# Attention with a top-32 mask and a routed feed-forward layer: rows scattered straight to their expert's place, and the end of a unit put behind the next search

## The chip, the cores and the metric

The kernel runs on one core of one Trainium2 chip. The metric is device time in microseconds (us) of one execution; the kernel before takes 1912.75 us, the median of three runs (1911.58 to 1913.21). TensorE (PE) multiplies matrices and loads its stationary operand separately (PEld), VectorE (DVE) and ScalarE (ACT) work element by element, GpSimd (POOL) does small work and issues the indirect transfers (scatters and gathers by a list of row numbers), SyncE (SP) issues the plain ones. PSUM is the memory that TensorE writes to.

## The reference

```python
# attention: B, H, S, D = 8, 8, 576, 64
scores = q @ k^T / sqrt(D)
kth = np.partition(scores, -32, axis=-1)[..., -32:-31]   # the 32nd largest of each row
scores = np.where(scores >= kth, scores, -1e9)
attn = softmax(scores)                                   # denominator + 1e-9
x = (attn @ v) laid out as [B*S, H*D] = [4608, 512]
# feed-forward: 8 experts, each row goes to one
logits = x @ w_gate                                      # [4608, 8]
e = argmax(logits, axis=1); gate = softmax(logits)[e]
out = gate * (relu(x @ w1[e]) @ w2[e])                   # w1 [8,512,1024], w2 [8,1024,512]
```

All of it is float32, the scores too, since the mask and the choice of the expert hang on exact comparisons.

## The kernel before, in words

**Attention.** The work goes batch by batch (8), in each batch by unit (4; a unit is a pair of heads), in each unit by group (5: four groups with one tile of 128 queries of either head, and a fifth, half as large, with the last 64 queries of both). One step of the main loop (lines 555 to 572) takes one group: `scores` of the next group (TensorE, copied out of PSUM by ScalarE, line 216), `weights` of this group, `close` of the group before. `weights` is the search: VectorE folds the 576 scores of a row into 288 pairs (`hl`, lines 232 and 233), finds the 32 largest in four rounds of `max` and `match_replace` (lines 240 to 253), and multiplies the exponentials by the mask, with the row sum as a by-product (line 269). The exponentials are ScalarE's (line 244), and their bias `nbias` is -scale times the largest score, a multiplication of two columns on GpSimd (line 242).

`close` transposes the weights on TensorE (`transposed`). With the last group of a unit `outputs` follows: `po`, the product with `v` (line 317), `px` and `pl`, its transposed form and the gate's logits (lines 322 to 335), and then VectorE's part, which scales by the row sums and adds up the logits (lines 302 to 306, and 324 to 347). The transposes, `po`, `px`, `pl` and `rank` all share one pool of two PSUM buffers (`bank`). In the loop the last group of a unit is closed after the search of the next unit's first group.

**Routing.** With the last unit of a batch `route` follows. It finds each row's expert, counts on TensorE (`rank`) how many rows went there before, and so gets a position for each row in its expert's list. Five indirect transfers on GpSimd scatter the row numbers into `lists` in memory (line 382); they write one tensor, and each waits for the one before. The rows of `x`, with the gate's factor as column 513, go to `x_rows` in the order of the tokens, as plain writes (lines 392 and 395). Lists and rows are filled beforehand with a number, or zeros, that stand for "no row".

**Blocks.** A block is 128 list places of one expert. There are 43 block slots. How many are sure to be full after each batch is known beforehand (2, 6, 11, 15, 20, 24 after the second to the seventh batch), and as many are worked on beside the attention of the batch that follows; the last 19 come after all attention. `load_block` loads the list of a block (`idx`, three buffers), the two weight matrices (2 MB each, two buffers each) and gathers the rows by the list (`xg`, two buffers, line 453). It is called for the block two ahead of the one begun. `block` is cut into 17 pieces: transposes of the rows (`xtp`, copied to `xTs`), 8 steps of the first product (`ph`, relu to `hT`), 8 of the second (`py`); at its end ScalarE applies the factor (`y`, line 486), and GpSimd scatters the rows to `out` by the list (line 487).

**Order.** Every engine runs its instructions in the order in which they stand in its queue, and DMAs issued by SP or GpSimd stand in these queues too, with what they wait for. The order is set when the program is built: a scheduler goes by the place of an instruction in the program, and lets later ones go ahead where, by its own durations, an engine would stand. So parts of two groups, or block pieces, stand between each other's instructions, and a wait that it did not foresee holds up all that stands behind.

If some rows can't be decided by the folded search, a second, exact version of everything runs behind the main part (line 585 on); with these inputs it doesn't run.

Of the kernel before, what the change touches and what calls it, by code (L numbers as in the profile page):

```python
# [9 lines left out]
F32 = mybir.dt.float32  # L10
# [3 lines left out]
AX = mybir.AxisListType  # L14

# [24 lines left out]
def kernel(  # L40
# [31 lines left out]

    nc = tc.nc
# [13 lines left out]
    XW = Dm + 1  # L87
    EB = N // P
    NSLOT = EB + E - 1
    LISTB = E * EB + NSLOT  # L90
# [35 lines left out]
    e_at = iota_f("e_at", [P, E], [[N, E]])  # L126
# [4 lines left out]

    tok_id = []
    for b in range(B):
        t = const.tile([P, KC], I32, name=f"tok_id{b}")
        token_ids(t, b)
        tok_id.append(t)
# [23 lines left out]
    lv = lists.rearrange("(r p) o -> p r o", p=P)  # L160
# [58 lines left out]
    def weights(n, tiles, s):  # L219
# [78 lines left out]
    def outputs(n, x, lg):  # L298
# [3 lines left out]
        if not k.exact:  # L302
            nc.vector.tensor_tensor(doubt, doubt, n.over, op=ALU.max)
        nc.vector.tensor_scalar_add(rz[:, 0:NT], n.z, EPS)
        nc.vector.reciprocal(rz[:, 0:NT], rz[:, 0:NT])
        nc.vector.tensor_copy(rz[0:ST, NT:NT + 1], rz[ST:P, NT - 1:NT])
# [12 lines left out]
        rzb = rz[:, :].rearrange("p (t h) -> p t h", h=2)  # L319
# [3 lines left out]
        xu = x[:, :, n.u * P:(n.u + 1) * P].rearrange("p t (h d) -> p t h d", h=2)  # L323
        nc.vector.tensor_tensor(
            xu[:, 0:NC], px[:, :].rearrange("p (t h d) -> p t h d", t=NC, h=2),
            _inner(rzb[:, 0:NC, :], D), op=ALU.mult,
        )
# [3 lines left out]
        for t in range(KC):  # L331
# [4 lines left out]
        nc.vector.tensor_tensor(  # L336
            xu[:, NC], pl[:, 0:P].rearrange("p (h d) -> p h d", h=2), _inner(rzb[:, NC, :], D), op=ALU.mult,
        )
        lt = k.small.tile([P, KC, 2, E], F32, name="lt")
        nc.vector.tensor_tensor(  # L340
            lt, pl[:, P:P + KC * lw].rearrange("p (t h e) -> p t h e", t=KC, h=2), _inner(rzb, E), op=ALU.mult
        )
        if n.u:
            nc.vector.tensor_tensor(lg, lg, lt[:, :, 0, :], op=ALU.add)
            nc.vector.tensor_tensor(lg, lg, lt[:, :, 1, :], op=ALU.add)
        else:
            nc.vector.tensor_tensor(lg, lt[:, :, 0, :], lt[:, :, 1, :], op=ALU.add)
# [309 lines left out]
```

## Time and profile before

| | |
|---|---|
| median of 3 runs | 1912.75 us |
| the profiled execution, its own time | 1911.04 us |
| its span, first to last instruction | 1909.3 us |
| mean granted TensorE clock | 0.825 of 2.4 GHz |
| TensorE busy | 1553.9 us, 81% |
| VectorE busy | 1421.3 us, 74% |
| ScalarE busy | 691.1 us, 36% |
| GpSimd busy | 222.7 us, 12% |
| mean DMA rate | 130 GB/s |

All times of the trace are from the profiled execution. A matmul's busy time includes time in the pipeline, so a busy TensorE is not one at its peak. An instruction's releaser (`<-`) is what it waited for last.

### The profile page before, as it was taken

The numbers are of one execution on the slowest core, as the hardware profiler recorded it, in microseconds if no ns is written. First come the engines' busy times: TensorE is split into PE (matmuls) and PEld (weight loads), VectorE is DVE, ScalarE is ACT, GpSimd is POOL, SyncE is SP. The second block draws the span as 40 slices with busy tenths as digits, with TensorE's granted clock in tenths as the row PEclk, the third lists the DMA queues.
The fourth block names the chain that finished last, engine by engine and source line by source line (L and its number), as shares of the span: only waits on it lengthen the run. The fifth ranks groups of instructions, "written<-read, shape, count | busy, mean of one in ns | idle before, by whom it ended". The sixth has DMA issues, their size and how long they took to land.

```text
span 1909.3 us, 25156 instructions
## 1 busy us (share of the span) xinstructions
PE 1553.9 (81%) x8126; PEld 993.1 (52%) x8126; DVE 1421.3 (74%) x4963; ACT 691.1 (36%) x1269; POOL 222.7 (12%) x471
## 2 busy tenths in 40 slices
PE   5778677877886699769996998599969973999998
PEld 3444344435543466446653664366536552666665
DVE  8999889997999799989997999799988970000000
ACT  3443243434443354434442453345434430111111
POOL 1000100011101110111011010211020101111110
PEclk9765666568956799779985998699959986999999
DMA  9300200015001551156315420644155206979884
GB/s 164 59 20 20 45 20 20 20 45 207 31 20 45 215 179 50 45 207 217 120 52 204 170 81 25 220 170 172 38 177 184 95 7 217 327 261 329 301 294 143
DMA packets 116525, 248.94 MB, mean 130 GB/s; under 512 B 12511, under 2 KB 33119, under 8 KB 116386
## 3 DMA queue, kind: packets, MB, share of 16 engines
q1 hardware_dynamic: 108226, 226.49, 36.5%
q0 software_dynamic: 8160, 20.76, 3.0%
q8 instruction: 67, 1.10, 0.2%
q14 instruction: 72, 0.59, 0.1%
HBM read 221.05 MB, written 28.01 MB: 130 GB/s over the span
## 4 chain that ended last, share of the span: by engine, by line
DVE 45%; PE 26%; DMA 14%; issue 10%; ACT 3%; POOL 2%; SPq 0%; POOLq 0%; DVEq 0%; ACTq 0%
DVE tops L240 13%; DVE scr L250 12%; PE po L317 9%; DVE w L269 7%; DMA out_dram<-y,idx 7%; PE sc L211 5%; PE ph L473 4%; DVE hl L232 3%; DVE tops L247 3%; DVE hl L233 3%; DMA idx<-lists 3%; DMA lists<-tok_id,posi 2%; DMA xg<-x_rows,idx 2%; PE wTm L283 2%; PE py L482 2%
## 5 line engine op out<-in xcount | busy, mean ns | idle before, releaser
L211 PE MATMUL sc<-qkb 64*128 64x288 f32 (+1 forms) x1280 | 379.5, 545 | 9.6 <-DMA qkb<-in_qk_dram 5.7
L473 PE MATMUL ph<-xTs,w 128*128 128x128 f32 x2752 | 348.2, 283 | 27.7 <-ACT xTs L465 27.4
L240 DVE MAX8 tops<-scr 128x8 f32<-128x288 f32 x864 | 356.1, 446 | 1.4
L283 PE MATMUL wTm<-ident,w 128*128 128x128 f32 x1152 | 226.8, 350 | 159.9 <-DVE w L269 150.5
L473 PEld LDWEIGHTS ph<-xTs,w 128*128 128x128 f32 x2752 | 328.7, 197 | 47.4 <-ACT xTs L465 39.8
L482 PE MATMUL py<-w,hT 128*128 128x512 f32 x688 | 315.6, 596 | 0.0
L283 PEld LDWEIGHTS wTm<-ident,w 128*128 128x128 f32 x1152 | 173.6, 180 | 239.3 <-issue 135.0
L244 ACT ACTIVATE w<-s,nbias 128x576 f32<-128x576 f32 x288 | 211.9, 773 | 229.4 <-POOL nbias L242 228.7
L250 DVE MATCH_REPLACE8 scr<-tops,scr 128x288 f32<-128x288 f32 x576 | 250.6, 440 | 0.1
L211 PEld LDWEIGHTS sc<-qkb 64*128 64x128 f32 (+1 forms) x1280 | 179.7, 221 | 130.2 <-issue 62.0
L216 ACT COPY s<-sc 128x576 f32<-128x576 f32 x288 | 174.0, 641 | 193.3 <-DVE w L269 105.8
L269 DVE SCALAR_TENSOR_TENSOR w<-s,thr,w 128x576 f32<-128x576 f32 x288 | 223.7, 807 | 12.5 <-ACT w L244 11.5
L286 ACT COPY wT<-wTm 128x512 f32<-128x512 f32 x256 | 142.7, 591 | 133.8 <-PE wTm L283 133.7
L482 PEld LDWEIGHTS py<-w,hT 128*128 128x128 f32 x688 | 122.3, 190 | 120.5 <-issue 120.3
L317 PE MATMUL po<-wT,vb 128*64 128x288 f32 x1024 | 158.5, 458 | 1.1 <-ACT wT L288 0.9
L232 DVE TENSOR_TENSOR hl<-s 128x576 f32<-128x576 f32 (+1 forms) x160 | 109.5, 685 | 63.9 <-ACT s L216 63.7
L240 DVE MAX8 tops<-hl 128x8 f32<-128x288 f32 x288 | 126.0, 448 | 0.0
L250 DVE MATCH_REPLACE8 scr<-tops,hl 128x288 f32<-128x288 f32 x288 | 125.7, 440 | 0.0
L265 POOL TENSOR_TENSOR over<-tops,thr 128x2 f32<-128x2 f32 (+1 forms) x160 | 36.5, 228 | 746.8 <-DVE thr L264 713.4
L291 PE MATMUL wTl<-ident,w 128*64 128x128 f32 x288 | 76.3, 347 | 55.3 <-ACT wT L286 54.6
L247 DVE MAX8 tops<-hl 128x8 f32<-128x288 f32 x288 | 120.6, 444 | 0.0
L317 PEld LDWEIGHTS po<-wT,vb 128*64 128x64 f32 x1024 | 75.4, 152 | 82.6 <-issue 40.4
(110 smaller groups left out, 1056.1 us busy)
## 6 DMA issues: line engine op xcount, KB each, us to landing
w<-in_moe_w_dram SPq DMA_DIRECT2D x86, 2048.0 KB
qkb<-in_qk_dram SPq DMA_DIRECT2D x32, 576.0 KB
vb<-in_v_dram SPq DMA_DIRECT2D x32, 320.0 KB
x_rows<-x SPq DMA_DIRECT2D x8, 1026.0 KB
x_rows<-zrow SPq DMA_DIRECT2D x1, 6925.5 KB
x_rows<-x SPq DMA_DIRECT2D x8, 128.2 KB
idx<-lists SPq DMA_DIRECT2D x43, 0.5 KB
xg<-x_rows,idx POOLq DMA_INDIRECT x43, 7.3
```

The source lines that it names most:

```text
L211: nc.tensor.matmul(ps[rows, j, 0:HF], n.q[d, cols], n.k[d, j * HF:(j + 1) * HF], start=True, stop=True)
L216: nc.scalar.copy(s[:, m, :, :], ps[:, :, 0:HF])
L232: nc.vector.tensor_tensor(hl[:, 0, m2, :], s[:, m2, 0, :], s[:, m2, 1, :], op=ALU.max)
L240: nc.vector.max(out=tops[:, m, r * 8:(r + 1) * 8], in_=src[m])
L244: nc.scalar.activation(w[:, m, :], flat[m], AF.Exp, scale=scale, bias=nbias[:, m:m + 1])
L247: nc.vector.max(out=tops[:, m, TOP_K + 1:TOP_K + 9], in_=hl[:, 1, m, :])
L250: nc.vector.match_replace(out=scr[:, m, :], in_to_replace=tops[:, m, r * 8:(r + 1) * 8], in_values=src[m], imm_value=NEG,)
L269: nc.vector.scalar_tensor_tensor(out=w[:, m, :], in0=flat[m], scalar=thr[:, m:m + 1], in1=w[:, m, :], op0=ALU.is_ge, op1=ALU.mult, accum_o ...
L283: nc.tensor.transpose(pm[:, c * P:(c + 1) * P], w[:, m, c * P:(c + 1) * P], ident)
L317: nc.tensor.matmul(po[r, 0:HF], lhsT, rhs, start=(c == 0), stop=(c == KC - 1))
L473: nc.tensor.matmul(ph[:, f, :], n.w1[:, 0, dt, fc * P:(fc + 1) * P], xT[:, dt, :], start=(dt == 0), stop=(dt == DT - 1),)
L482: nc.tensor.matmul(py, hT[:, f, :], n.w2[:, 0, f, :], start=(f == 0), stop=(f == FT - 1))
```

## The change

Eight edits.

1. `x_rows` becomes the experts' own stretches: each expert has `CAP` = 4736 rows there. A row has 514 columns: 512 values, the factor, and the number of the token (as an integer). `lists` is gone, and so are the fills at the start.
2. `route` scatters whole rows (five indirect transfers, 128 or 64 rows of 2056 bytes) to their positions. The five are declared independent of one another.
3. `load_block` loads 128 consecutive rows with one plain transfer on SP, which waits for all the scatters. There is no `idx`: the output is scattered by the row tile's last column. The row tile has two buffers, as before.
4. `fill_up`, new, runs after the last batch: one block of blank rows behind each expert's last row, and an `EMPTY` block that the slots past the last are sent to.
5. `outputs` is cut in two: TensorE's and ScalarE's part stays, VectorE's part is returned as `scaled`.
6. `settle`, new, calls `scaled`, and for a batch's last unit `route`, the table of blocks and the loads. The loop calls it right after the next group's `weights` and before `close`, so VectorE's part of a unit comes one search later than before.
7. `nbias` is computed on ScalarE.
8. In the last batch the pieces that are dealt out among the groups leave two blocks (`KEEP`), which come in the program behind the last unit and ahead of the last 19.

```diff
-    XW = Dm + 1
+    XW = Dm + 2
-    LISTB = E * EB + NSLOT
+    CAP = N + P
+    EMPTY = E * CAP // P
...
-    x_rows = dram.tile([N + 1, XW], F32, name="x_rows")
-    lists = dram.tile([LISTB * P, 1], I32, name="lists")
+    x_rows = dram.tile([(EMPTY + 1) * P, XW], F32, name="x_rows")
...
-                nc.gpsimd.tensor_scalar(nbias[:, m2], tops[:, m2, 0], -scale, None, ALU.mult)
+                nc.scalar.mul(nbias[:, m2], tops[:, m2, 0], -scale)
...
-    def outputs(n, x, lg):
+    def outputs(n):
...
+        def scaled(x, lg):
+            if not k.exact:
+                nc.vector.tensor_tensor(doubt, doubt, n.over, op=ALU.max)
+            nc.vector.tensor_scalar_add(rz[:, 0:NT], n.z, EPS)
...
+        return scaled
...
-        for i in range(KC):
-            r = slice(0, P if i < NC else ST)
-            nc.gpsimd.indirect_dma_start(
-                out=lists[:, :], out_offset=bass.IndirectOffsetOnAxis(ap=posi[r, i:i + 1], axis=0),
-                in_=ids[r, i:i + 1], in_offset=None,
-            )
...
-        nc.sync.dma_start(
-            x_rows[bass.ds(row0, SM), :].rearrange("(c p) w -> p c w", p=P), x[:, 0:NC, :]
-        )
-        nc.sync.dma_start(x_rows[bass.ds(row0 + SM, ST), :], x[0:ST, NC, :])
+        mine = []
+        for i in range(KC):
+            r = slice(0, P if i < NC else ST)
+            put = nc.gpsimd.indirect_dma_start(
+                out=x_rows[:, :], out_offset=bass.IndirectOffsetOnAxis(ap=posi[r, i:i + 1], axis=0),
+                in_=x[r, i, :], in_offset=None,
+            ).ins
+            if not k.exact:
+                for other in mine:
+                    tc.declare_no_dep(put, other, reason="the rows of one batch go to different places")
+                mine.append(put)
+        scattered.extend(mine)
+
+    def fill_up():
+        ends = k.small.tile([1, E], I32, name="ends")
+        nc.vector.tensor_copy(ends, run[0:1, :])
+        for e in range(E):
+            r = nc.sync.value_load(ends[0:1, e:e + 1], min_val=e * CAP, max_val=e * CAP + N)
+            put = nc.sync.dma_start(x_rows[bass.ds(r, P), :], blank).ins
+            if not k.exact:
+                for other in scattered:
+                    tc.add_manual_dep(put, other.name, WAIT)
+        nc.sync.dma_start(x_rows[EMPTY * P:(EMPTY + 1) * P, :], blank)
...
-        n.idx = k.mlp.tile([P, 1, 1], I32, name="idx", bufs=3)
-        nc.sync.dma_start(n.idx, lv[:, bass.ds(r, 1), :])
+        n.x = k.mlp.tile([P, 1, XW], F32, name="xg")
+        got = nc.sync.dma_start(n.x, xv[:, bass.ds(r, 1), :]).ins
+        if not k.exact:
+            for put in scattered:
+                tc.add_manual_dep(got, put.name, WAIT)
         n.w1 = k.wp.tile([P, 1, DT, F], F32, name="w1")
...
-        n.x = k.mlp.tile([P, XW], F32, name="xg")
-        nc.gpsimd.indirect_dma_start(
-            out=n.x[:, :], out_offset=None,
-            in_=x_rows[:, :], in_offset=bass.IndirectOffsetOnAxis(ap=n.idx[:, 0, 0:1], axis=0),
-        )
...
         nc.gpsimd.indirect_dma_start(
-            out=out[:, :], out_offset=bass.IndirectOffsetOnAxis(ap=n.idx[:, 0, 0:1], axis=0),
+            out=out[:, :], out_offset=bass.IndirectOffsetOnAxis(ap=n.x[:, 0, Dm + 1:XW].bitcast(I32), axis=0),
             in_=y[:, :], in_offset=None, bounds_check=N - 1, oob_is_err=False,
         )
...
+    FIRST = 5
+    KEEP = 2 * PIECES
...
-            if g != groups[-1]:
+            if g == groups[-1]:
+                late = (b, u, outputs(n))
+
+        def settle():
+            nonlocal late, left
+            if late is None:
                 return
+            b, u, scaled = late
+            late = None
...
-            outputs(n, x_of[b], lg_of[b])
+            scaled(x_of[b], lg_of[b])
             if u < U - 1:
                 return
-            route(x_of[b], lg_of[b], tok_id[b], b * S)
+            route(x_of[b], lg_of[b])
+            if b == B - 1:
+                fill_up()
...
             w = weights(n, g, s_now)
+            settle()
             if last is not None:
                 close(last)
             last = (b, u, g, w)
             at = i % per_batch
-            if at >= 5:
-                pieces(-(-left // (per_batch - at)))
+            if at >= FIRST:
+                rest = left - (KEEP if b == B - 1 else 0)
+                pieces(-(-rest // (per_batch - at)))
         close(last)
+        settle()
         pieces(left)
```

## Rows read from the trace of the kernel before

**Rows 1.** The page: busy time by engine, slices, and the costliest group's line.

```profile
PE 1553.9 (81%) x8126; PEld 993.1 (52%) x8126; DVE 1421.3 (74%) x4963; ACT 691.1 (36%) x1269; POOL 222.7 (12%) x471
...
DVE  8999889997999799989997999799988970000000
...
L211 PE MATMUL sc<-qkb 64*128 64x288 f32 (+1 forms) x1280 | 379.5, 545 | 9.6 <-DMA qkb<-in_qk_dram 5.7
```

**Rows 2.** Stretches from unit to unit: length, busy time (instructions), clock, DMA.

```profile
10.40:57.66 47.26, 31.18 (x98) 17.18 (x96) 47.23 (x159) 19.95 (x36) 2.68 (x11) 1.00 1.01 134
...
150.27:197.02 46.75, 38.39 (x142) 20.94 (x144) 43.36 (x147) 18.41 (x34) 2.44 (x10) 0.57 0.07 20
197.02:252.23 55.21, 34.59 (x147) 19.60 (x148) 45.52 (x167) 18.62 (x35) 8.29 (x15) 0.62 0.18 39
...
651.87:695.49 43.62, 42.78 (x258) 28.05 (x260) 42.74 (x145) 21.39 (x39) 4.69 (x12) 1.00 0.59 202
...
1177.76:1238.28 60.52, 36.63 (x188) 24.49 (x190) 46.63 (x183) 19.68 (x37) 11.86 (x17) 0.66 0.50 161
...
sum 1552.95, PE 1257.83 PEld 781.40 DVE 1411.24 ACT 642.60 POOL 176.87; mean PE 39.31 PEld 24.42 DVE 44.10 ACT 20.08 POOL 5.53
```

**Rows 3.** Waits of VectorE, 10.4 to 1563.35 us: total us, times, longest.

```profile
DVE hl L232 <- ACT s L216: 59.1, 17, 10.2
DVE x L324 <- PE px L322: 47.7, 18, 6.2
DVE w L269 <- ACT w L244: 11.5, 5, 4.2
DVE x L336 <- PE pl L332: 11.0, 22, 1.4
DVE base L367 <- PE rank L363: 4.7, 7, 0.9
```

**Rows 4.** Timeline of GpSimd and ScalarE: first batch's end, start and length.

```profile
236.82 0.92 POOL L382 DMA_INDIRECT lists<-tok_id,posi  x1 [2.04 <-DMA lists<-tok_id,posi]
237.77 0.24 POOL L242 TENSOR_SCALAR nbias<-tops 128x2 f32<-128x2 f32 x1
...
238.04 1.44 ACT L244 ACTIVATE w<-s,nbias 128x576 f32<-128x576 f32 x2 [9.80 <-POOL nbias L242]
```

**Rows 5.** Timeline at the sixth batch's end, all engines.

```profile
1190.47 0.24 ACT L387 ACTIVATE lg<-lg 128x40 f32<-128x40 f32 x1 [2.58 <-DVE lg L386]
...
1196.47 0.17 DVE L379 CAST posi<-posf 128x5 int32<-128x5 f32 x1 [0.41 <-DVE both L260]
...
1217.00 0.64 PE L291 MATMUL wTl<-ident,w 128*64 128x128 f32 x2 [3.21 <-ACT wT L286]
...
1226.05 1.12 PE L463 MATMUL xtp<-ident,xg 128*128 128x128 f32 x4 [8.41 <-DMA xg<-x_rows,idx]
...
1230.05 0.76 DVE L232 TENSOR_TENSOR hl<-s 128x576 f32<-128x576 f32 x1 [9.37 <-ACT s L216]
```

**Rows 6.** Waits of the whole kernel, TensorE's for gathered rows.

```profile
PE xtp L463 <- DMA xg<-x_rows,idx: 76.9, 7, 29.8
```

**Rows 7.** Timeline from the last unit to the first tail block.

```profile
1571.49 0.69 DVE L324 TENSOR_TENSOR x<-px,rz 128x512 f32<-128x512 f32 x1 [9.39 <-PE px L322]
...
1577.86 0.17 DVE L379 CAST posi<-posf 128x5 int32<-128x5 f32 x1
...
1606.07 1.11 PE L463 MATMUL xtp<-ident,xg 128*128 128x128 f32 x4 [29.79 <-DMA xg<-x_rows,idx]
...
1607.86 8.95 PE L473 MATMUL ph<-xTs,w 128*128 128x128 f32 x64 [0.68 <-ACT xTs L465]
```

**Rows 8.** The list scatters: issue time on GpSimd, ns min/median/max.

```profile
L382 POOL DMA_INDIRECT lists<-tok_id,posi x40: 902/1004/2260, 216.8 to 1594.5; - x40
```

**Rows 9.** The output's scatters (line 487): from issue to landing.

```profile
DMA to landing us min/median/max: 2.1/6.6/9.1
```

**Rows 10.** Tail: timeline of one block, and its piece of the chain of waits.

```profile
1663.34 7.03 PE L482 MATMUL py<-w,hT 128*128 128x512 f32 x16
...
1671.41 0.95 POOL L453 DMA_INDIRECT xg<-x_rows,idx  x1 [13.27 <-ACT y L486]
...
1671.68 7.41 PE L473 MATMUL ph<-xTs,w 128*128 128x128 f32 x64 [0.87 <-ACT xTs L465]
...
1672.67 1.02 POOL L487 DMA_INDIRECT out_dram<-y,idx  x1 [0.30 <-issue]
...
1679.73 1.96 DMA idx<-lists
...
1889.84 7.41 PE L473 MATMUL ph<-xTs,w 128*128 128x128 f32 x64 [0.86 <-ACT xTs L465]
```

**Rows 11.** Stretches of the tail, columns as in rows 2 (last two DMA share, GB/s).

```profile
1632.00:1640.00 8.00, 7.64 (x24) 3.53 (x22) 0.00 (x0) 1.30 (x3) 0.00 (x0) 1.00 0.95 362
1640.00:1890.00 250.00, 235.64 (x1345) 169.84 (x1346) 0.00 (x0) 38.16 (x65) 32.38 (x33) 1.00 0.82 290
```

**Rows 12.** The row gathers (line 453): from issue to landing.

```profile
DMA to landing us min/median/max: 5.5/7.3/8.6
```

More of the change, by code (lines that the diff above doesn't have):

```diff
@@ L130, in token_ids @@
         nc.gpsimd.iota(t, pattern=[[P, KC]], base=b * S, channel_multiplier=1)
[L132 to L136, printed above, removed]
     NTOP = 4
@@ L159 @@
     w2v = moe_w2.rearrange("e (ft p) d -> p e ft d", p=P)
-    lv = lists.rearrange("(r p) o -> p r o", p=P)
+    xv = x_rows.rearrange("(r p) w -> p r w", p=P)
+    blank = const.tile([P, XW], F32, name="blank")
+    nc.gpsimd.memset(blank[:, 0:Dm + 1], 0.0)
+    nc.gpsimd.iota(blank[:, Dm + 1:XW].bitcast(I32), pattern=[[0, 1]], base=N, channel_multiplier=0)
+    scattered = []
     groups = [(i, NC + i) for i in range(NC)] + [(2 * NC,)]
@@ L391, in route @@
         nc.vector.reciprocal(x[:, :, Dm], den)
-        nc.sync.dma_start(
-            x_rows[bass.ds(row0, SM), :].rearrange("(c p) w -> p c w", p=P), x[:, 0:NC, :]
-        )
-        nc.sync.dma_start(x_rows[bass.ds(row0 + SM, ST), :], x[0:ST, NC, :])
-    def empty_lists(pool):
-        pad = pool.tile([P, LISTB], I32, name="pad", bufs=1)
-        nc.gpsimd.iota(pad, pattern=[[0, LISTB]], base=N, channel_multiplier=0)
-        nc.sync.dma_start(lists.rearrange("(p f) o -> p (f o)", p=P), pad)
+        mine = []
[20 more added lines that the diff above has]
+        nc.sync.dma_start(x_rows[EMPTY * P:(EMPTY + 1) * P, :], blank)
     def table(n, last):
@@ L432, in table @@
         )
+        if last:
+            none = sm.tile([1, NSLOT], F32, name="none")
+            nc.vector.tensor_scalar(none[:, 0:n], slots[:, 0:n], upto[:, E - 1:E], float(EMPTY), ALU.is_ge, ALU.mult)
+            nc.vector.tensor_tensor(slot_f[:, 1, 0:n], slot_f[:, 1, 0:n], none[:, 0:n], op=ALU.max)
+            nc.vector.tensor_scalar_min(slot_f[:, 1, 0:n], slot_f[:, 1, 0:n], float(EMPTY))
         slot_i = sm.tile([1, 2, NSLOT], I32, name="slot_i")
@@ L493 @@
     PIECES = 2 + 2 * FT - 1
+    FIRST = 5
+    KEEP = 2 * PIECES
     with ExitStack() as st:
         open_pools(st, False)
-        zrow = const.tile([P, XW], F32, name="zrow")
-        nc.gpsimd.memset(zrow, 0.0)
         unit_of = {(0, 0): load_unit(0, 0)}
-        empty_lists(const)
-        late = next(b for b in range(B) if sure[b]) + 1
-        nc.sync.dma_start(
-            x_rows[late * S:N, :].rearrange("(c p) w -> p c w", p=P), _ins(zrow[:, :], 1, (N - late * S) // P)
-        )
-        nc.sync.dma_start(x_rows[N:N + 1, :], zrow[0:1, :])
         work = [(b, u, g) for b in range(B) for u in range(U) for g in groups]
@@ L532, in close @@
         def close(last):
-            nonlocal left
+            nonlocal late
             b, u, g, w = last
@@ L590 @@
             token_ids(ids, 0)
-            empty_lists(keep)
             nc.vector.tensor_copy(run, e_at)
```

63 lines of the change are left out of this document (33 added, 30 removed).

## The prediction

> **What bounds the kernel now.** I read the page first: VectorE is busy 1421.3 us, and its row of slices is full up to slice 33 and then empty [rows 1]. So there are two stages: attention, bound by VectorE's top-32 search, and behind about 1571 us a tail in which only the last 19 expert blocks are left and TensorE sets the time. Next I cut attention at the first `po` matmul of each unit. All stretches together are 1552.95 us long with VectorE busy 1411.24 [rows 2]: 141.7 us of idle time is all that the first stage can give. A unit without blocks is 46.8 us long with 43.4 of VectorE's work; the unit across the end of a batch is 55.2 and 45.5, or 60.5 and 46.6 where blocks start; in a unit full of blocks TensorE is busy 42.8 of 43.6 us.
>
> VectorE's waits name the idle time [rows 3]: 59.1 us for the score copies of ScalarE, 47.7 for `px` and 11.0 for `pl` (the end of a unit: VectorE comes to read its products while TensorE is still making them, in 18 and 22 of 31 units), 11.5 for the exponentials, 4.7 for the rank. Two of these have causes further back. The exponentials wait for `nbias`, which stands on GpSimd behind five list scatters that wait for one another: at 236.82 the fifth goes out, at 237.77 `nbias` runs, and ScalarE had then stood 9.80 us [rows 4]. The score copies wait in ScalarE's queue behind `xTs`, that is behind the first block's rows: positions are known at 1196.64, TensorE has nothing left before `xtp` at 1217.64, the rows come at 1226.05, and VectorE stands 9.37 us [rows 5]. Over the kernel `xtp` waits 76.9 us in seven places [rows 6]; without the last (29.79 us, the start of the tail [rows 7]) that is 47.1 in six batches, 7.9 each.
>
> **The change part by part.** The sum is made against the span of the profiled execution, 1909.3 us; its own time is 1911.04 (1.7 around the span) and the median of the runs 1.7 above that.
>
> *VectorE's end of a unit, one search later.* `px` is ready 2.6 us, on average, after VectorE now asks for it (47.7 / 18), and the next search takes about 9.2 us (43.4 of a unit less some 2 for its end, over four double groups and a single one). Moved behind it, the 58.7 us of rows 3 go to nothing in the 31 units that have a next search; the last unit has none and keeps its 9.39 us [rows 7]. No instruction is added. The cover is the search itself; if the order that is built put these steps back into its gaps, all 58.7 would return. **-58.7.**
>
> What is late next: `px` and `pl` are the two buffers of the pool that the transposes of the weights also use. They are now held through one more search, and TensorE may do only scores (379.5 us for 160 groups [rows 1], 2.4 each) and block pieces there, then two groups' transposes in a row. Nothing in the trace shows this. Bounds: 0, or 9.2 - 2.4 = 6.8 us in each of 31 units, 211 us. In sparse units there is room (38.4 of 46.8 us busy), in dense ones 258 instructions against 142, so over a hundred block instructions to fill the hole with [rows 2]. I take 0.8 us in each of 12 dense units: **+10**, close to the lower end since something is at hand to run in both kinds.
>
> *`nbias` on ScalarE.* GpSimd no longer stands between search and exponential: the 11.5 us of rows 3 go. 160 activations are added, by the nearest small one 0.24 us each [rows 5], 38 us on an engine that is busy 36% [rows 1], in a place where it stands waiting anyway. **-11.5**; without that cover up to 38 back.
>
> *Rows scattered straight, blocks as plain loads.* Now, from positions to rows: 1226.05 - 1196.64 = 29.4 us (five scatters one after the other, an index load, a gather). Then: five scatters issued at 1.0 us each [rows 8], 5.0; the last lands after 6.6 as the output's scatter of the same size does (2.1 to 9.1 [rows 9]); a plain load, 0.35 to issue, 2.0 as the index load [rows 10], and 263 KB at 362 GB/s [rows 11], 0.7. Sum 14.7 us; with the ends of the rows 10 to 24. But TensorE's queue is an order written down at build time, and it will ask earlier too. It now asks 21.0 us after the positions, 71% of the chain; 71% of 14.7 is 10.5, and 4.2 us of wait are left of 8.4. Bounds: the place stays at 21 us and the 47.1 go, or it moves up to 6 us and all stay. I take half: **-24**. The row writes, index loads, lists and the zero rows that leave SP's queue save nothing: the zero rows go out while VectorE is at 47.23 of 47.26 us [rows 2].
>
> By *DMA: Bandwidth & Descriptors* of the Trainium skill, section "Anatomy of one DMA — SWDGE (gpsimd) path", a GpSimd transfer costs about 2.0 us plus its bytes at 436 GB/s, by which I estimate 2.6 us for these 263 KB; the gather of that size took 7.3 in the median [rows 12], so the trace does not agree. By the page the chain would be 10.7 us and the boundary stalls gone, 23 us below my sum.
>
> *Start of the tail.* Now the first tail block's `ph` starts 36.4 us after `px` (1571.49 to 1607.86 [rows 7]). Then: positions at 1578.0, scatters issued by 1583.0, landed 1589.6; nine blank fills, 2.4 MB at 362 GB/s and 2.0, 1598.1; the rows and behind them the first weights, 0.35 + 2.0 + 0.7 + 5.8: 1607.0. Two blocks are held back for this gap (2 x 15.6 = 31 us of TensorE). Whether they run there or are drawn forward into the last batch as pieces are now, `ph` of the first tail block starts at 1607: **0**; bounds -2 (the first block's `ph` in 7.41 us as later ones, for 8.95) and +10 (scatters that land after 9.1, fills that queue).
>
> *The tail's loop.* 14 blocks from 1671.68 to 1889.84 are 15.58 us each, TensorE without a hole but for one copy. The index list had three buffers; now the index lies in the row tile, which has two, so the rows of block j+2 wait for the output scatter of block j, and on SP both weight loads queue behind them. From the end of `py` (1670.37): scatter issued 1.0 later (the gather that stood before it is gone), landing 7.1 later as in rows 10 (1672.67 to 1679.73), t + 8.1; rows and first weights 8.9 later, t + 17.0. TensorE wants these weights at t + 1.3 + 15.58 = t + 16.9. Level, then; each microsecond more costs half a microsecond a block, 9.5 over 19. I take a landing 0.7 us later, for the rows, weights and scatter that now come together: **+7**; bounds 0 and, at 9.1 plus 2 of queueing, +38.
>
> Sum: 1909.3 - 58.7 + 10 - 11.5 - 24 + 0 + 7 = 1832; with what lies around the span 1834; on the median of the runs **1835**.
>
> **Rivals.**
> *Banks.* TensorE can't use the hole while `px` and `pl` wait, and scores come late in each unit: 211 us against the 94 gained: 1835 + 211 - 10, some 2036. For: dense units have 0.8 us of slack. Against: over a hundred block instructions per dense unit that don't need that pool. It decides from 2.8 us per unit ((58.7 + 11.5 + 24 - 7) / 31); slower than before.
> *The tail waits.* Output scatters land at 9 and queue 2 us: period 17.5, 1835 + 31 = 1866. For: the DMA engines are already busy 82 to 95% here [rows 11]; against: they keep pace now.
> *All waits go.* 141.7 less the 4.7 for the rank and a few: -130 and 0 in the tail, 1783 to 1795.
> *It doesn't do it.* VectorE's steps are put back beside `px`, TensorE asks as early as before: only `nbias` is left, 1905 to 1915.
> *Starved scatters.* GpSimd makes the descriptors of 2 KB rows slowly beside a busy VectorE: 2.26 us an issue (the longest of rows 8) and 9.1 to land: chain 23.4, nine longer in each of six batches, 52 of wait: 1835 + 52 = 1887. Median issue is 1.0 in either stage, which speaks against.
>
> *SBUF — State Buffer* of the Trainium skill, section "SBUF: two separate sides", says that GpSimd can't write descriptors while VectorE holds the port that both share; this is that rival's rule, and the median of rows 8 shows little of it.
>
> **How the numbers follow.** Forecast 0.45 (own range 1805 to 1860), all waits go 0.15, tail 0.12, starved 0.08, not done 0.08, banks 0.12. The range takes in the forecast, the second, the tail, the starved case and the near half of "not done": 1775 to 1908, with 0.16 to 0.2 outside. About 0.2% (4 us) is what can be told from no change; faster holds the first four, 0.80; "not done" splits into 0.05 same and 0.03 slower; slower 0.15 with the banks.
>
> **What would show it.** No wait for `px` before the last unit; units without blocks at 43 to 44 us (right), at 46 and more with score waits (banks). No ScalarE wait for GpSimd. `xtp` waits of about 4 us at six places. Last `px` read at about 1487. Tail period 15.6 to 16; a wait of `ph` for weights would be the loop. The prediction falls if units get longer than 45 us without blocks, or the tail's period passes 17.

## The result, and the profile after

The changed kernel takes 1796.72 us (median of 4 runs, 1791.09 to 1798.92). The kernel before took 1912.98 us beside it. The ratio is 0.9386 with a 95% interval of 0.9362 to 0.941: 6.1% faster. The forecast was 1835, with a range from 1775 to 1908; the time lies below the likeliest case's own range (1805 to 1860) and just above the rival in which all waits go (1783 to 1795). The profiled execution took 1796.5 us, its span is 1794.8 against 1909.3.

From the page of the changed kernel: busy time by engine, VectorE's slices.

```profile
PE 1530.6 (85%) x8126; PEld 978.2 (55%) x8126; DVE 1416.3 (79%) x4967; ACT 721.7 (40%) x1429; POOL 121.1 (7%) x268
...
DVE  8999999999999999999999999999999920000000
```

Against [rows 1], VectorE does the same work (1416.3 for 1421.3 us), but the sevens in its row are gone, and its last slice with work, the 33rd in both, shows a 2 for a 7. TensorE still does its 8126 matmuls; GpSimd lost half its time, and ScalarE gained 30.6 us by 160 activations, 0.19 us each.

Stretches of the changed kernel, columns as in [rows 2] (length, then busy time and instructions of PE, PEld, DVE, ACT, POOL; clock, DMA share, GB/s): all attention units, a unit without blocks, the one across the first batch's end, a unit full of blocks, the one in which the sixth batch ends and blocks start.

```profile
10.40:1442.92 1432.52, 1233.79 (x6459) 765.79 (x6455) 1406.62 (x4908) 673.16 (x1347) 95.31 (x225) 0.84 0.29 105
144.44:187.73 43.29, 32.05 (x142) 17.36 (x141) 43.18 (x147) 19.58 (x39) 0.96 (x5) 0.70 0.07 22
187.73:233.60 45.87, 34.97 (x146) 20.26 (x145) 45.13 (x167) 19.80 (x40) 6.29 (x11) 0.61 0.14 47
588.43:633.01 44.58, 44.58 (x267) 29.74 (x265) 44.02 (x148) 22.59 (x46) 1.97 (x6) 0.96 0.59 217
1080.91:1127.71 46.80, 37.09 (x184) 23.98 (x183) 45.70 (x180) 20.37 (x42) 6.49 (x11) 0.67 0.43 151
```

The unit without blocks fell from 46.75 to 43.29 us, of which VectorE works 43.18: nothing is left to gain there. The end of the first batch fell from 55.21 to 45.87, the sixth's from 60.52 to 46.80. Over all units 1432.52 - 1406.62 = 25.9 us of VectorE's idle time remain of 141.7. The full unit is now TensorE's, busy 44.58 of 44.58 us; with 267 matmul instructions for 258 it is no shorter than the one of [rows 2] (43.62).

VectorE's waits in this stretch (total us, times, longest), as in [rows 3]:

```profile
DVE hl L233 <- ACT s L217: 14.5, 14, 4.0
DVE base L373 <- PE rank L369: 4.0, 7, 0.6
DVE w L270 <- ACT w L245: 0.3, 1, 0.3
```

`px` and `pl` no longer stand here at all; over the whole kernel `px` is waited for once, at the last unit. The largest fall besides is that of the score copies, 59.1 to 14.5.

The sixth batch's end, the timeline of all engines, as in [rows 5]:

```profile
1104.10 0.15 DVE L385 CAST posi<-posf 128x5 int32<-128x5 f32 x1
...
1104.52 1.00 POOL L395 DMA_INDIRECT x_rows<-x,posi  x1 [12.08 <-DVE full L428]
...
1110.22 0.90 POOL L395 DMA_INDIRECT x_rows<-x,posi  x1 [0.30 <-issue]
...
1113.11 0.36 SPq L467 DMA_DIRECT2D xg<-x_rows  x1
...
1115.99 1.12 PE L481 MATMUL xtp<-ident,xg 128*128 128x128 f32 x4 [3.85 <-DMA xg<-x_rows]
...
1117.15 0.59 ACT L483 COPY xTs<-xtp 128x512 f32<-128x512 f32 x1 [5.08 <-PE xtp L481]
...
1119.08 1.19 ACT L217 COPY s<-sc 128x576 f32<-128x576 f32 x2
...
1120.30 0.76 DVE L233 TENSOR_TENSOR hl<-s 128x576 f32<-128x576 f32 x1 [0.33 <-ACT s L217]
```

From positions (1104.25) to `xtp` it is 11.7 us instead of 29.4. TensorE asks for the rows at 1112.14, 7.9 us after the positions, where it asked after 21.0. It waits 3.85, and VectorE 0.33 for the copies behind `xTs`. The other five places look the same: TensorE waits 3.7 to 5.5 us, VectorE then 0.32 or 0.33.

Over the whole kernel the rows are waited for 26.3 us in six batches (50.6 less the last):

```profile
PE xtp L481 <- DMA xg<-x_rows: 50.6, 7, 24.3
```

From the last unit to the tail, and one block of the tail with the last one, as in [rows 7] and [rows 10]:

```profile
1451.07 0.69 DVE L336 TENSOR_TENSOR x<-px,rz 128x512 f32<-128x512 f32 x1 [8.94 <-PE px L318]
...
1462.91 0.90 POOL L395 DMA_INDIRECT x_rows<-x,posi  x1 [0.30 <-issue]
...
1466.54 4.96 SPq L411 DMA_DIRECT2D x_rows<-blank  x8
...
1480.17 1.12 PE L481 MATMUL xtp<-ident,xg 128*128 128x128 f32 x4 [24.33 <-DMA xg<-x_rows]
...
1486.00 9.79 PE L491 MATMUL ph<-xTs,w 128*128 128x128 f32 x64 [4.71 <-DMA w<-in_moe_w_dram]
...
1503.66 1.00 POOL L505 DMA_INDIRECT out_dram<-y,xg  x1 [39.85 <-ACT y L504]
1503.91 7.41 PE L491 MATMUL ph<-xTs,w 128*128 128x128 f32 x64 [0.82 <-ACT xTs L483]
...
1507.46 0.35 SPq L467 DMA_DIRECT2D xg<-x_rows  x1
...
1768.78 7.41 PE L491 MATMUL ph<-xTs,w 128*128 128x128 f32 x64 [0.86 <-ACT xTs L483]
```

**Where the 114.5 us of span went.** The last `px` is read at 1451.07 instead of 1571.49: -120.4. From there to the first tail `ph` it is 34.9 us instead of 36.4: -1.4. From that to the last `ph` 282.8 instead of 282.0 (1889.84 - 1607.86): +0.8. From the last `ph` to the end of the span 26.0 instead of 19.5: +6.5. In the sum these were -84.2 (three terms and the bank price), 0, +7 and 0.

### The profile page after: what moved, and what is told of

Read it like the earlier page. It is cut to its first block, busy times and chain, and to the rows that moved or that the text cites. A ratio compares the mean times of both kernels' runs of the same rounds, so it can differ in the third digit from the quotient of the medians.

```text
span 1794.8 us, 24778 instructions
## 1 busy us (share of the span) xinstructions
PE 1530.6 (85%) x8126; PEld 978.2 (55%) x8126; DVE 1416.3 (79%) x4967; ACT 721.7 (40%) x1429; POOL 121.1 (7%) x268
## 5 line engine op out<-in xcount | busy, mean ns | idle before, releaser
L212 PE MATMUL sc<-qkb 64*128 64x288 f32 (+1 forms) x1280 | 375.2, 540 | 47.3 <-ACT s L217 40.8
L491 PE MATMUL ph<-xTs,w 128*128 128x128 f32 x2752 | 343.9, 282 | 29.1 <-ACT xTs L483 24.1
L284 PE MATMUL wTm<-ident,w 128*128 128x128 f32 x1152 | 216.2, 336 | 108.6 <-DVE w L270 84.9
L284 PEld LDWEIGHTS wTm<-ident,w 128*128 128x128 f32 x1152 | 166.0, 173 | 181.8 <-ACT nbias L243 44.6
L212 PEld LDWEIGHTS sc<-qkb 64*128 64x128 f32 (+1 forms) x1280 | 174.5, 217 | 165.1 <-ACT s L217 71.1
L496 ACT ACTIVATE hT<-ph 128x512 f32<-128x512 f32 x86 | 51.4, 598 | 206.8 <-PE ph L491 206.5
L233 DVE TENSOR_TENSOR hl<-s 128x576 f32<-128x576 f32 (+1 forms) x160 | 109.5, 684 | 19.9 <-ACT s L217 19.9
L234 DVE TENSOR_TENSOR hl<-s 128x576 f32<-128x576 f32 (+1 forms) x160 | 110.0, 688 | 0.0
## 6 DMA issues: line engine op xcount, KB each, us to landing
w<-in_moe_w_dram SPq DMA_DIRECT2D x86, 2048.0 KB, 12.5
```

The costliest lines, as they stand in the source:

```text
L212: nc.tensor.matmul(ps[rows, j, 0:HF], n.q[d, cols], n.k[d, j * HF:(j + 1) * HF], start=True, stop=True)
L284: nc.tensor.transpose(pm[:, c * P:(c + 1) * P], w[:, m, c * P:(c + 1) * P], ident)
L491: nc.tensor.matmul(ph[:, f, :], n.w1[:, 0, dt, fc * P:(fc + 1) * P], xT[:, dt, :], start=(dt == 0), stop=(dt == DT - 1),)
```

## The experiments

The first chip gave the result above; the others ran on chips on which the kernel before took 1925.84 to 1928.35 us. The changed kernel took 1799.12 there (e5, below). Runs e1 to e4 shared one chip, e5 to e8 another, e9 to e11 a third. A variant is compared with e5 by its time, and with the kernel before on its own chip by its ratio; a difference of a few us between two of these chips is to be read with the ratios beside it. The only trace of the kernel before is from the first chip. Where waits of e6 to e8 are set against it, they are set against a run that was some 14 us faster than the kernel before on their own chip.

| run | median us | ratio to before, 95% |
|---|---|---|
| e1_end_back | 1864.32 | 0.9665 [0.9647, 0.9683] |
| e2_nbias_back | 1808.40 | 0.9366 [0.9341, 0.9391] |
| e3_none_kept | 1793.80 | 0.9296 [0.9278, 0.9314] |
| e4_three_row_tiles | 1798.06 | 0.9328 [0.9312, 0.9344] |
| e5_changed_again | 1799.12 | 0.9349 [0.9315, 0.9384] |
| e6_end_alone | 1872.87 | 0.9738 [0.9702, 0.9775] |
| e7_rows_alone | 1863.02 | 0.9682 [0.9646, 0.9718] |
| e8_nbias_alone | 1914.26 | 0.9942 [0.9925, 0.9959] |
| e9_index_copied | 1804.86 | 0.9373 [0.936, 0.9386] |
| e10_early_fills | 1787.24 | 0.9271 [0.9255, 0.9288] |
| e11_weights_first | 1788.78 | 0.9291 [0.9277, 0.9305] |

**The end of a unit back in front of the next search.** In the loop `settle()` runs after `close`, that is where the old code had it:

```diff
-            settle()
             if last is not None:
                 close(last)
+            settle()
```

> The changed kernel with one thing undone: VectorE's part of a unit comes again right behind TensorE's part, ahead of the next search. Theory (each wait has its own price): the waits for px and pl come back in 31 units, 58.7 us as before the change, so 1797 + 59 = 1855 us; VectorE's waits for px and pl show 50 to 65 us before the last unit, units without blocks are 46 us long. Rival (the gain is not in these waits but in rows, blocks and nbias, since VectorE's place in the queue only moves a stall to the next search): under 15 us lost, 1800 to 1812, and the waits for ScalarE's score copies take the place of those for px.

It took 65 us more than e5, or 61 by the ratios. VectorE's waits over the whole kernel:

```profile
DVE hl L233 <- ACT s L217: 45.2, 11, 6.3
DVE x L336 <- PE px L318: 39.3, 13, 8.8
DVE x L340 <- PE pl L323: 10.4, 26, 0.4
```

`px` and `pl` are back with 49.7 us where e5 has 7.7; before the last unit it is 40.5 us, less than the 50 to 65 that were expected. The score copies grew from 22.2 in e5 to 45.2. So the edit is worth 42 us of its own wait and 23 us of another one, together the 65 us of the time. Beside it TensorE's wait for the rows rose to 46.2 in the six batches. How the one leads to the other was not taken apart.

**`nbias` back on GpSimd.**

```diff
-                nc.scalar.mul(nbias[:, m2], tops[:, m2, 0], -scale)
+                nc.gpsimd.tensor_scalar(nbias[:, m2], tops[:, m2, 0], -scale, None, ALU.mult)
```

> The changed kernel with nbias computed on GpSimd again. Theory: the price was GpSimd standing behind list scatters that wait for one another; now the five scatters of a batch don't, they take GpSimd about 5 us in a row, so little comes back: 0 to 5 us, 1797 to 1802, with ScalarE's longest wait for nbias under 6 us (9.8 before). Rival (the hop to GpSimd costs in each search, whatever stands there): the 11.5 us come back, 1808.

It took 9.3 us more than e5, close to what the rival expected. The two ran on different chips and the intervals of their ratios overlap; against e4, which ran on the same chip and takes no longer than the changed kernel (below), it is 10.3 us more, every run above every run of e4. ScalarE's wait for GpSimd, whole kernel:

```profile
ACT w L245 <- POOL nbias L243: 188.7, 94, 4.2
```

No wait is longer than 4.2 us, where the one behind the list scatters was 9.80 [rows 4]; 94 short ones make up the sum. VectorE does not wait for the exponentials, but its score copies come late more often, 30.0 us instead of 22.2, and the last `px` later, 9.8 instead of 7.3. These 10.3 us are about what the span gained (1807.2 for 1797.2). So with the lists gone the way over GpSimd still costs. That it does so because ScalarE makes the exponential and the next score copy in turn is argued, not shown.

**No block held back for the tail.**

```diff
-    KEEP = 2 * PIECES
+    KEEP = 0
```

> The changed kernel with no blocks held back for the tail (all pieces dealt out in the last batch). Theory (the order that is built draws the two kept blocks forward anyway: TensorE stands 24.3 us for rows at the start of the tail of the changed kernel too): no change beyond 3 us, 1794 to 1800, first tail ph still 35 us after the last px. Rival (keeping two blocks lightens the last batch or fills the start of the tail): 8 to 30 us slower, 1805 to 1827.

The time fell by 5.3 us against e5, which ran on another chip (the intervals of the ratios just part), and by 4.3 against e4 on its own. In the changed kernel TensorE stood 24.33 us idle at `xtp` although two blocks were held back for that place: they had been drawn forward. Without them the first tail `ph` comes 36.4 us after the last `px`, with them 34.9 to 36.1. What is held back buys nothing. The gain of e3, if it is one, lies ahead of the tail: its last `px` is read at 1447.47, that of e5 at 1451.80.

**Three row tiles.** The tile of rows and indices gets a third buffer, so that the rows of block j+2 no longer wait for the output of block j.

```diff
-        n.x = k.mlp.tile([P, 1, XW], F32, name="xg")
+        n.x = k.mlp.tile([P, 1, XW], F32, name="xg", bufs=3)
```

> The changed kernel with three buffers for a block's rows, so that rows and weights of block j+2 no longer wait for the output scatter of block j. All queues but SP's have the same order. Theory (the scatter lands in under 4 us in the changed kernel because that wait keeps the weight loads off the DMA engines while it runs; before, with weights in flight, it took 6.6): the scatters land in 5 to 7 us again in the tail, the tail's period stays 15.58 us, time unchanged within 4 us. Rival (the scatter is faster for another reason, such as the index lying in the row tile): landing stays under 4 us. Second rival (the wait costs TensorE time): 3 to 10 us faster.

The time is the same within its interval, and the tail's period is 15.58 us in both. The wait that the change added to SP's queue costs no time. The stretch 1600 to 1760 of this run, then of the changed kernel:

```profile
1600.00:1760.00 160.00, 151.35 (x879) 110.21 (x879) 0.00 (x0) 24.17 (x41) 9.85 (x10) 1.00 0.86 303
```

```profile
1600.00:1760.00 160.00, 151.35 (x880) 110.21 (x879) 0.00 (x0) 24.17 (x41) 9.83 (x10) 1.00 0.81 298
```

The weights landed 9.4 us after issue in the median instead of 12.5, and the engines were busier for about the same bytes. Nothing waits for the output scatter here, so no line of the profile has its landing, but the traces have its DMA packets. From the scatter's issue to the end of its last packet, the first 16 scatters of the tail take 7.1 us in the median in this run (5.9 to 8.6), 2.7 in the changed kernel (2.0 to 3.9), 2.5 in e5 and 7.0 in the kernel before. So the third buffer alone brings the slow landing back, as the theory said. The index lies in the row tile here as in the changed kernel, so that rival falls: it is the company of the weight loads that makes the scatter slow.

**The changed kernel again**, on the chip of the next three.

> The changed kernel as it is, as the measure for those run on this chip beside it. Theory: 1790 to 1800 us here as on the first chip, since its time hangs on VectorE's own instructions and TensorE at full clock; the kernel before, which waits more on transfers, may differ by some 15 us from chip to chip. Rival: its ratio to the kernel before is a constant of the change, 0.936 to 0.941 on any chip.

1799.12 us, 2.4 more than on the first chip, while the kernel before went up by 14. VectorE's wait for score copies is 22.2 for 19.9, the six waits for rows are 23.8.

**Each part alone, on the kernel before.** First, only the end of a unit moved: `outputs` returns its VectorE half, and `settle` runs it after the next search.

```diff
-    def outputs(n, x, lg):
+    def outputs(n):
...
+        def scaled(x, lg):
...
+        return scaled
...
-            outputs(n, x_of[b], lg_of[b])
+            scaled(x_of[b], lg_of[b])
```

> The kernel before with one edit alone: VectorE's part of a unit behind the next search; lists, gathers and nbias on GpSimd as before. Theory (the waits for px and pl are a price of their own): 59 us faster than the kernel before, 0.969; no wait for px before the last unit. Rival (the parts need one another: routing that comes one search later meets list scatters that still take 29 us, and the blocks' rows come later still): under 40 us faster, and xtp waits of 8 us or more in six batches.

-54 us, where 59 were expected. VectorE and the rows in this run, whole kernel:

```profile
DVE hl L232 <- ACT s L216: 85.4, 27, 9.8
DVE x L335 <- PE px L317: 8.6, 1, 8.6
...
PE xtp L468 <- DMA xg<-x_rows,idx: 66.2, 7, 34.0
```

`px` is left to the last unit alone, units without blocks are 43.3 us long, but a batch's end still takes 55.5 to 59.3 us, and the score copies there come later than in the trace of the kernel before (85.4 for 63.7). Against that trace VectorE's waits for `px`, `pl`, exponentials and score copies fall by 45.5 us in all, and the span by 42.0.

Then the rows alone: the changed kernel with `settle()` behind `close`, `nbias` on GpSimd and `KEEP = 0`, as in the three diffs above together.

> The changed kernel with only the rows scattered straight and the blocks as plain loads: VectorE's end of a unit, nbias and the dealing of pieces as before the change. Theory: the chain from positions to rows is 14 us for 29, which gives about 39 us of the score-copy waits plus the part of the nbias wait that came from scatters waiting for one another: 40 to 50 us faster than the kernel before, 0.974 to 0.979. Rival (only the end of a unit and nbias count; TensorE asks for the rows so much earlier that its wait stays): under 20 us faster, xtp waits of 7 to 8 us in six batches. GpSimd's drain at the very end is 6 to 7 us long if whole rows through GpSimd's transfers make it so, 1 to 2 if not.

-64 us, more than either theory expected; the interval is some 7 us either way. Its waits:

```profile
DVE hl L233 <- ACT s L217: 42.4, 12, 6.1
DVE x L336 <- PE px L318: 41.2, 14, 9.3
DVE x L340 <- PE pl L323: 11.3, 28, 0.4
...
PE xtp L481 <- DMA xg<-x_rows: 72.3, 7, 25.3
```

TensorE waits for rows as long as ever, 47.0 us in six batches: it asks just as much earlier as the rows come (4.7 to 6.6 us after the positions for 20.7 to 24.1, and the rows are there after 12.5 to 15.6 for 28.3 to 31.9). And still VectorE's wait for score copies fell by 21 us, that for `px` by 16, and the one for the exponentials (11.5) is gone with the lists, though `nbias` is on GpSimd here. That is 48.7 us in all against the trace of the kernel before, whose span is 48.6 longer; what the other 15 us of the -64 were can't be read, as no trace of the kernel before is from this chip. So the rows' part pays through a shorter way from a batch's end to its blocks, which TensorE's own wait does not show.

Then `nbias` alone, by the diff of e2 in the other direction.

> The kernel before with nbias on ScalarE alone. Theory: the 11.5 us of waits for the exponentials go, and at the first batch's end the wait of ScalarE with them: 10 to 14 us faster than the kernel before, 0.993 to 0.995. Rival (VectorE then meets the same places in the score copies, which stand behind xTs): 0 to 5 us faster. Second rival (160 activations on ScalarE cost): slower by up to 10.

-12.4 us. Its waits:

```profile
DVE hl L232 <- ACT s L216: 81.0, 11, 15.1
DVE x L324 <- PE px L322: 54.5, 17, 9.6
...
PE xtp L463 <- DMA xg<-x_rows,idx: 125.2, 7, 33.0
```

The wait for exponentials (11.5) is gone, and that for score copies rose from 63.7 to 81.0, with 92 us of TensorE's waits for rows in six batches instead of 47.1. TensorE asks for the rows 14.6 to 17.9 us after the positions here instead of 20.7 to 24.1, and they come no sooner (31.0 to 34.8 for 28.3 to 31.9). By the sum of VectorE's waits (+17.3 for score copies, -2.5 for `px`, -1.5 for `pl`, -11.5) this run should be 1.8 us longer than the trace of the kernel before, and its span is 2.6 longer (1911.9 for 1909.3). So the waits agree with the span; the 12.4 us are against the kernel before on this chip, of which no trace was kept, and which of its waits they were can't be read.

The three alone make -54 - 64 - 12 = -130; together, on the same chip, they make 1799.12 - 1926.69 = -127.6. The parts add up within their intervals (7, 7 and 3 us either way, and 7 for the whole). e7 also has no blocks held back, which is worth some 4 us by itself (e3).

**The end of the span.** Of the 6.5 us at the end, 5.3 go to a drain, an instruction of GpSimd's queue behind the last block. The last drains in the changed kernel (ns, shortest, median, longest, then start of the first and last), and in the kernel before:

```profile
L678 POOLq DRAIN  x3: 40/107/6843, 1787.1 to 1794.5; - x3
```

```profile
L652 POOLq DRAIN  x3: 40/107/1564, 1906.9 to 1909.1; - x3
```

The drain is 6.84 to 6.86 us in all ten profiles of kernels that scatter rows (the changed kernel and e1 to e11 but for e6 and e8) and 1.4 to 1.8 in the three that scatter lists (before, e6, e8). One guess was the output scatter, which now reads its indices from a strided column of the row tile. e9 copies them to a tile of their own:

```diff
+        idx = k.mlp.tile([P, 1], I32, name="idx")
+        nc.gpsimd.tensor_copy(idx, n.x[:, 0, Dm + 1:XW].bitcast(I32))
...
-            out=out[:, :], out_offset=bass.IndirectOffsetOnAxis(ap=n.x[:, 0, Dm + 1:XW].bitcast(I32), axis=0),
+            out=out[:, :], out_offset=bass.IndirectOffsetOnAxis(ap=idx[:, 0:1], axis=0),
```

> The changed kernel with the index column copied into a small tile of its own by GpSimd when a block begins; the output scatter reads the copy, so a row tile comes free at the block's end, without the scatter. Theory A (GpSimd's drain at the very end, 6.84 us for 1.56 before the change, is long because the last scatter reads its index out of the wide row tile): drain under 2 us, 5 to 6 us faster, about 1792. Theory B (it comes with row scatters through GpSimd, or from another part of the program): drain still 6.8 us, time within 3 us of 1797. For the output scatters: rows still wait for nothing but the block, so weights are in flight beside the scatter and it lands in 5 to 8 us in the tail, as in the run with three row tiles.

The drain stays at 6.85 us, so the guess falls. The time is 5.7 us above that of e5, on another chip and with intervals that overlap, and VectorE got a new wait for GpSimd of 8.9 us in all. What the drain waits for stays open: row scatters, plain row loads and blank fills came in together, and no run takes them apart.

On the output scatters e9 agrees with e4. GpSimd's next copy waits for the scatter to land, here some 8 us after its issue, with the weight loads beside it (by the packets 7.2 us in the median):

```profile
1601.43 0.98 POOL L507 DMA_INDIRECT out_dram<-y,idx  x1 [9.06 <-ACT xTs L485]
1609.54 0.18 POOL L483 COPY idx<-xg 128x1 int32<-128x1 int32 x1 [7.12 <-DMA out_dram<-y,idx]
```

**A version that beats both.** The blank fills (eight that end each expert's stretch, one for empty slots) wait for the last row scatter, although no row goes where they write. In e10 they go out as soon as the counts are known, and the loads wait for both; no block is held back.

```diff
-    KEEP = 2 * PIECES
+    KEEP = 0
...
-                for other in scattered:
-                    tc.add_manual_dep(put, other.name, WAIT)
+                for other in scattered + filled:
+                    tc.declare_no_dep(put, other, reason="behind the last row of each expert")
+                filled.append(put)
...
+            scattered.extend(filled)
```

> The changed kernel with no blocks held back, and with the blank fills independent of the scatters (they go behind each expert's last row, where no scatter writes), so that they run beside the scatters and not behind them. Theory (the start of the tail is a chain: positions, scatters, fills, rows, weights, each waiting for the one before): the first rows are loaded about 10 us sooner after the last px, first tail ph 24 to 26 us after it instead of 35; 1784 to 1790 us. Rival (the fills' 2.4 MB then stand in the way of the scatters, and all land together): 2 us or less gained, 1792 to 1798.

It is the fastest, 1787.24 us, ratio 0.9271, clear of e5. Against e3, which also holds nothing back, the intervals of the ratios overlap (0.9255 to 0.9288, 0.9278 to 0.9314), so what the early fills are worth is read from the traces. The start of the tail here:

```profile
1449.83 0.69 DVE L336 TENSOR_TENSOR x<-px,rz 128x512 f32<-128x512 f32 x1 [8.64 <-PE px L318]
...
1456.00 10.46 SPq L412 DMA_DIRECT2D x_rows<-blank  x8
...
1469.93 0.35 SPq L474 DMA_DIRECT2D xg<-x_rows  x1
...
1472.79 1.11 PE L488 MATMUL xtp<-ident,xg 128*128 128x128 f32 x4 [18.62 <-DMA xg<-x_rows]
...
1478.51 8.97 PE L498 MATMUL ph<-xTs,w 128*128 128x128 f32 x64 [4.61 <-DMA w<-in_moe_w_dram]
```

The fills start at 1456.00, before the positions' scatters are through; the first `ph` comes 28.7 us after `px` where 24 to 26 were expected; it was 34.9 in the changed kernel and 36.4 in e3, so the fills give some 7.7 us. The eight fills hold SP for 10.46 us now instead of 4.96, as each needs a count read into a register first: in the changed kernel SP read the eight counts from 1457.5 to 1461.7, while it would have waited for the scatters anyway, and here the reads stand between the fills.

The last step was the 4.61 us that the first `ph` then waits for its weights: e11 loads the first half of them ahead of the rows.

```diff
+        if first:
+            load_w1()
         n.x = k.mlp.tile([P, 1, XW], F32, name="xg")
```

> As the run with early fills, and the first tail block loads its first weight matrix ahead of its rows, since the weights need only the table of blocks, some 9 us after the last px. Theory (the weights' 6 to 8 us leave the chain): first tail ph 20 to 23 us after the last px, 2 to 5 us faster than with early fills alone. Rival (2 MB on the same engines hold up fills and rows by as much): no gain, or 1 to 3 us slower than early fills alone.

No gain: 1788.78 us. The wait only moved, from the weights to the rows:

```profile
1447.41 0.69 DVE L336 TENSOR_TENSOR x<-px,rz 128x512 f32<-128x512 f32 x1 [8.81 <-PE px L318]
...
1466.23 0.41 SPq L474 DMA_DIRECT2D w<-in_moe_w_dram  x1
...
1475.12 1.11 PE L495 MATMUL xtp<-ident,xg 128*128 128x128 f32 x4 [22.93 <-DMA xg<-x_rows]
...
1476.91 10.31 PE L505 MATMUL ph<-xTs,w 128*128 128x128 f32 x64 [0.68 <-ACT xTs L497]
```

The first `ph` comes 29.5 us after `px`, against 28.7.

## Why the prediction was right, and where its sizes were not

The direction, the places and the mechanism of the gain held; the time came out 38 us lower than the sum, and one step, from TensorE's wait for the rows to VectorE's, was wrong. By its terms:

| term | sum | measured in the two profiles |
|---|---|---|
| `px`, `pl` | -58.7 | -58.7 |
| banks | +10 | 0 |
| `nbias` | -11.5 | -11.2 |
| rows, by the score copies | -24 | -44.6 |
| VectorE's busy time | 0 | -4.6 |
| tail's start | 0 | -1.4 |
| tail's loop | +7 | +0.8 |
| end of the span | 0 | +6.5 |

With the rank (-0.7) and the last unit (-0.4) these give -114.3 of -114.5. VectorE's work itself is no shorter: its instructions in this stage are the same in number, and their own times add up to 1723.5 and 1723.0 us. They overlap a little more, and so the time in which VectorE is busy is 4.6 us less.

*`px` and `pl`* went as said: not one such wait before the last unit. e1 brings 42 us of them back, e6 takes them away alone (-54 us).

*Banks.* I put 0.8 us on each of 12 dense units, close to the lower end. The lower end was right, or near it: a price would show as late score copies, and 14.5 us of these are left in all. Units without blocks are 43.3 us long, in the changed kernel and in e6. In the full unit TensorE is busy without a gap (44.58 of 44.58 us), so there it found work for the time in which the two buffers were held.

*`nbias`.* The size was right on the kernel before: e8 measures -12.4 for -11.5. The wait that was its reason is gone there, but others grew, so that the size came from this reason is not shown. In the changed kernel it isn't the reason: with no list scatters there is no long wait (none over 4.6 us in e7), and e2 has 94 short ones of ScalarE.

*Rows: the mis-sized term.* The chain was 11.7 us for 14.7: five scatters landed after 3.0 us in the median, not 6.6, and the load after 2.8. TensorE asks after 7.9 us where I put 10.5, and the wait that is left is 26.3 / 6 = 4.4 us a batch, for 4.2. All that was near. Wrong was the step from there to the time: I gave VectorE the same wait that TensorE keeps, by analogy with [rows 5], where 8.41 of the one stood beside 9.37 of the other. At the sixth batch's end TensorE now waits 3.85 us and VectorE 0.33, and the other five are like it.

The order of the queues isn't the reason: in both kernels the score copies that VectorE needs next stand behind `xTs` on ScalarE and are done about 4 us after `xtp` starts. What counts is when VectorE needs them. In the kernel before it had searched all that it had 24.0 us after the positions (1230.05 - 9.37 - 1196.64). TensorE asked after 21.0, so even rows that lay ready would have brought the copies too late (21.0 + 4.0), and all of TensorE's wait passed to VectorE. Now VectorE is through its last group, the short fifth one of the unit, 15.7 us after the positions (1120.30 - 0.33 - 1104.25). TensorE asks after 7.9, so the copies could be there after 12.2, and the first 3.5 us of its 3.85 pass while VectorE has work. So 45 of the 59.1 went. (Not all 45 need be the rows': e2 shows the way of `nbias` in the score copies as well, 30.0 for 22.2.) e7 says the same in part: with TensorE's wait unchanged at 47.0, the late score copies that follow the six waits take 27.2 us from VectorE, where in the kernel before they took 44.3. The rival in which all waits go was, in the first stage, the better forecast: -120.4 for its -130.

On the landing of a scatter, *DMA: Bandwidth & Descriptors* of the Trainium skill, section "Anatomy of one DMA — SWDGE (gpsimd) path", gave an estimate of 2.6 us, and the gathers of [rows 12] spoke against it with 7.3. Here the trace agrees with the page, 2.6 to 3.9 with 3.0 in the median: the difference lay in the company, not in the path. By the packets, the row scatters met none of SP's transfers, while each of the 43 gathers ran beside weight loads, in the tail (6.4 to 8.6 us) and beside attention (5.5 to 8.0) alike. The output's scatters in the kernel before say the same: the 14 that met none of SP's transfers landed after 2.1 to 4.5 us, the other 29 after 4.9 to 9.1.

*Tail's start.* It is 34.9 us for 36.4, but the chain in it came out by luck: the scatters have landed 14.7 us after `px` where I put 18.1, and the fills then take 11.6 us until the first rows are loaded where I put 8.5. That the held blocks might be drawn forward was left open; they were (24.33 us of idle TensorE), and e3 shows them to be worth nothing.

*Tail's loop.* The +7 was not paid: the period is 15.58 in both kernels. I let the output scatter land after 7.1 us [rows 10], but the wait that the change adds keeps the next block's loads behind it, so that it has the DMA engines nearly to itself: its landing is 2.8 in the median where it was 6.6 [rows 9]. The DMA share in the stretch of one such landing, in the changed kernel and before (the last two columns):

```profile
1503.60:1507.40 3.80, 3.49 (x31) 3.49 (x32) 0.00 (x0) 0.26 (x1) 1.00 (x1) 1.00 0.17 63
```

```profile
1672.70:1679.70 7.00, 7.00 (x60) 6.61 (x59) 0.00 (x0) 1.17 (x2) 0.99 (x1) 1.00 0.93 330
```

That the quiet makes it fast, and that the wait costs nothing, are both shown by e4.

*End of the span.* Not in the sum at all: a drain of 6.84 us, cause open.

The rivals: no sign of starved scatters, with issues of 897 to 1311 ns and landings of at most 3.9; the tail waits for weights once, 4.7 us at its first block; and the change does what it says, as VectorE's steps did not return to their gaps.

## What to carry to other kernels

A reader that comes too early is cheapest cured by work that doesn't need its data: 58.7 us of waits went by moving VectorE's steps behind the next search, at no price that the traces show, though two shared buffers stay full for longer. Before a wait of one engine is charged to the engine that sets the time, look at when the latter needs what stands behind that wait: here VectorE had a short group left to search, and 3.85 us of TensorE's wait cost it 0.33. Take the duration of a transfer from rows that stand in the same company (2.8 to 3.0 us in quiet, 6.6 to 7.3 beside weight loads, the same bytes), and ask of an added wait what it keeps out of the way.

## What was not expected of the hardware

GpSimd's drain at the end takes 6.84 to 6.86 us in the ten kernels that scatter rows, 1.4 to 1.8 in the three that scatter lists. The kernel before takes 13 to 15 us more on three other chips than on the first, the changed one 2.4 more on the one where it ran again: ratios from different chips (0.9386 and 0.9349 for the same two kernels) agree to 0.4%, not better. And a fill issued on SP whose count is read into a register just before it took 10.46 / 8 = 1.3 us in e10, where eight with the counts read ahead took 4.96 together.
